# Attention with beacon tokens and an MLP on one core: values loaded straight to their rows, smaller first loads, and a fixed order of products per pair

## The chip, the cores and the metric

The kernel runs on one core of one Trainium2 chip. The metric is the device time of one execution in microseconds. An engine works through its own instruction list in order; engines meet through semaphores. The engines are TensorE (PE, matrix products), VectorE (DVE), ScalarE (ACT), GpSimd (POOL, which also issues the loads that change fp32 into fp16) and SyncE (SP, which issues the other DMAs).

## The reference

There are 8 batches of 8 heads, 576 tokens each, head width 64, and 16 beacon keys and values ahead of the tokens of each head. After the attention, an MLP (512 to 2048 to 512) runs over the 4608 tokens.

```python
k_all = np.concatenate([beacon_k, k], axis=2)      # 592 keys
v_all = np.concatenate([beacon_v, v], axis=2)
scores = scale * np.matmul(q, k_all.transpose(0, 1, 3, 2))
scores = np.where(causal, -1000000000.0, scores)   # beacons always seen
a = softmax(scores)
attn = np.matmul(a, v_all)
x = attn.transpose(0, 2, 1, 3).reshape(B * S, H * D)
h = x @ w_in
out = (h * (1.0 / (1.0 + np.exp(-1.702 * h)))) @ w_out
```

## The kernel before, in words

**Attention.** A step is one pair of heads of one batch: 32 steps. Scores are computed transposed, keys on the partitions (five blocks of 128 rows, the beacons being the first 16), in four chunks per pair (`qk_chunk`, L346). ACT takes the exponential of each chunk into an fp16 tile `E` (L364; two of them), and POOL or DVE clears the causal blocks. `av_half` (L413) multiplies by the values, four times per pair, into PSUM tiles `u` (four in the ring); the value tile holds ones beside the values, so the sums come out with the products. DVE or ACT evicts them to `O` (three); DVE alone turns the sums, takes reciprocals, turns them back, and multiplies into `xT` (L445 to L472).

**MLP.** Tokens are taken in nine groups of 512. The first layer has 16 tiles per group (`mlp1`, L489), each followed by a Gelu on ACT (L502), the second layer four tiles (`mlp2`, L512). ACT loads another table when it changes between exponential and Gelu. Group `g` becomes due behind step `ends[g]` (L806), 6, 10, 14 and so on.

**Queries and keys.** For batches 0 and 1 they are loaded six tokens to a row (`load_qk6`, L148) and transposed on PE (`tr_pe`, L174). For later batches they are loaded in another form (`load_qk`, L130), turned in squares on DVE (L273), put in order by DVE or POOL (L282), written to DRAM and read back in place by SP (L294 to L306).

**Values.** For batches 2 to 7 six DMAs per batch (`load_v`, L231) put each head's 64 values of a row straight in place. For batches 0 and 1 the values are loaded six tokens to a row into space that w_out will occupy later (`load_v6`, L160), and PE moves them to their rows with products against a 0/1 matrix (`v_pe`, L204; 30 products per batch and one for the beacons), which ACT or DVE evict (`v_pe_out`, L224). So three of the four loads of w_out wait for the last of these products (L702).

**The order.** Each piece of work is a `Work` with engines and estimated durations, a key, needs, and pieces that must be issued before it (`after`). `issue` (L849) simulates the engines: it takes again and again the piece that can start earliest, at equal times the one with the lowest key, and the instructions are then issued in that order. PSUM and SBUF tiles are handed out in rings (`Buf`, L551), so a piece may have to wait for the users of an older tile. Nothing but keys, needs and rings orders the products of PE among each other. Loads of later batches also wait for a step's first exponential (`late`, L706). Where the simulated PE would be idle in the first 60 us, it may put in warm-up products (`warm`, L914).

Of the kernel before, what the change touches and what calls it, by code (L numbers as in the profile page):

```python
# [16 lines left out]
def kernel(  # L17
# [11 lines left out]
    nc = tc.nc  # L29
# [22 lines left out]
    NBV = 2  # L52
# [27 lines left out]
    make_identity(nc, ident)  # L80
    keep = cst.tile([P, P + Nb], F16, tag="keep", name="keep")
    spread = cst.tile([TP, NKPAD + TR + 2], F16, tag="spread", name="spread")
    bkn = cst.tile([Nb, NB2, H, D], F16, tag="bkn", name="bkn")
    bvn = cst.tile([Nb, NBV, H, D], F16, tag="bvn", name="bvn")
# [13 lines left out]
    def make_spread():  # L98

        nc.gpsimd.affine_select(  # L100
            out=spread,
            in_=spread,
            compare_op=ALU.not_equal,
            fill=1.0,
            base=-Nb - TR,
            pattern=[[1, NKPAD + TR + 2]],
            channel_multiplier=-TR,
        )

# [9 lines left out]

# [3 lines left out]
    for t in kTs:  # L123
        nc.vector.memset(t[:, :, NK:NKPAD], 0.0)
# [21 lines left out]
    vflat = w2t.rearrange("p a n -> p (a n)")  # L146

    def load_qk6(b, g, w):  # L148
        if b not in nat6:
            nat6[b] = gp.tile([TP, 2, H, TR * D], F16, tag="g", name="g")  # L150
        nc.gpsimd.dma_start(
            out=nat6[b][:, w, g * HG : (g + 1) * HG, :],
            in_=(q, k)[w][b, g * HG : (g + 1) * HG].rearrange("h (p t) d -> p h (t d)", t=TR),
        )

    def v6(b):
        n = H * TR * D
        return vflat[0:TP, b * n : (b + 1) * n].rearrange("p (h t d) -> p h t d", h=H, t=TR)

    def load_v6(b):  # L160
        nc.gpsimd.dma_start(
            out=v6(b).rearrange("p h t d -> p h (t d)"),
            in_=v[b].rearrange("h (p t) d -> p h (t d)", t=TR),
        )

    def load_beacons(t, src):
        nc.gpsimd.dma_start(
            out=t.rearrange("n b h d -> n (b h) d"),
            in_=src[0 : t.shape[1]].rearrange("b h n d -> n (b h) d"),
        )  # L170
# [30 lines left out]

    vu = {}

    def v_pe(b, j):  # L204
        u = psu.tile([P, H * D], F32, tag="u", name="u")
        vu[(b, j)] = u
        if j == 0:
            nc.tensor.matmul(
                u[:, :],
                ident[0:Nb, :],  # L210
                bvn[:, b, :, :].rearrange("n h d -> n (h d)"),
                start=True,
                stop=False,
            )
        for t in range(TR):
            nc.tensor.matmul(  # L216
                u[:, :].rearrange("r (h d) -> r h d", h=H),
                spread[:, j * P - t + TR : (j + 1) * P - t + TR],
                v6(b)[:, :, t, :],
                start=(t == 0 and j > 0),  # L220
                stop=(t == TR - 1),
            )

    def v_pe_out(b, j, eng):  # L224
        r = min(P, NK - j * P)
        copy[eng](
            out=vbs[b % 2][0:r, j, :, 0:D],
            in_=vu[(b, j)][0:r, :].rearrange("r (h d) -> r h d", h=H),
        )

    def load_v(b, j, h0, h1):  # L231
        vb = vbs[b % 2]
        if j == 0:
            nc.gpsimd.dma_start(
                out=vb[0:Nb, 0, h0:h1, 0:D],
                in_=beacon_v[b, h0:h1].rearrange("h n d -> n h d"),
            )
            nc.gpsimd.dma_start(
                out=vb[Nb:P, 0, h0:h1, 0:D],
                in_=v[b, h0:h1, 0 : P - Nb, :].rearrange("h n d -> n h d"),  # L240
            )
        else:
            lo = j * P - Nb
            hi = min(lo + P, S)
            nc.gpsimd.dma_start(  # L245
                out=vb[0 : hi - lo, j, h0:h1, 0:D],
                in_=v[b, h0:h1, lo:hi, :].rearrange("h n d -> n h d"),
            )
# [311 lines left out]
    SEM = 0.1  # L560
# [10 lines left out]
    mkeep = Work("POOL", 0.3, -4.75, make_keep)  # L571
    mspread = Work("POOL", 1.0, -4, make_spread)
    beac = []

    def first_loads(b):
        k0 = 4 * b
        kl = -5 + 0.4 * b
        gb6 = Buf("g")
        lds = {}
        for g in range(2):  # L580
            for w in (1, 0):
                lds[(g, w)] = Work(
                    "POOL", 0.7, kl + 0.1 * g, lambda b=b, g=g, w=w: load_qk6(b, g, w),
                    alloc=gb6 if not lds else None, dma=1.8, after=list(lds.values())[:1],
                )
            if b == 0 and g == 0:
                for (t, src) in ((bkn, beacon_k), (bvn, beacon_v)):
                    beac.append(Work(
                        "POOL", 0.56, kl + 0.05, lambda t=t, src=src: load_beacons(t, src), dma=0.6,
                    ))  # L590
        ub = Buf("u")
        x = Work("PE", 0.3, k0, lambda b=b: tr_pe_beacon(b), beac[:1], alloc=ub)
        y = Work("DVE", 0.25, k0, lambda b=b: tr_pe_beacon_out(b), [x], alloc=kTb[b])
        use(ub, y)
        for p in range(NPAIR):
            for w in (1, 0):
                ub = Buf("u")
                kk = 4 * b + p - 0.5
                x = Work(
                    "PE", 0.55, kk, lambda b=b, p=p, w=w: tr_pe(b, p, w), [lds[(p // 2, w)]],  # L600
                    alloc=ub, after=[x],
                )
                use(gb6, x)
                z = Work(
                    dict(ACT=0.66, DVE=0.76), 0, kk,
                    lambda eng, b=b, p=p, w=w: tr_pe_out(b, p, w, eng),
                    [x], alloc=qTb[b] if (w, p) == (0, 0) else None,
                    after=[y] if w == 1 else [pk[(b, 0, 0)]] if p else (),
                )
                use(ub, z)  # L610
                pk[(b, p, w)] = z
        pk[b] = y

    def first_values(b):
        lv = Work("POOL", 0.8, -4.8, lambda b=b: load_v6(b), dma=3.6)
        for j in range(NJ):
            ub = Buf("u")
            kk = 4 * b + 0.5
            x = Work("PE", 1.35, kk, lambda b=b, j=j: v_pe(b, j), [lv, mspread] + beac[1:], alloc=ub,
                after=vpe[-1:],  # L620
            )
            V[(b, j)] = Work(
                dict(ACT=0.6, DVE=0.68), 0, kk,
                lambda eng, b=b, j=j: v_pe_out(b, j, eng),
                [x], alloc=vbb[b] if j == 0 else None, after=[V[(b, 0)]] if j else (),
            )
            use(ub, V[(b, j)])
            vpe.append(x)

    vpe = []  # L630
    for b in range(B):
# [5 lines left out]
        for g in range(2) if b >= NB2 else ():  # L637
            for w in (1, 0):
# [3 lines left out]
                    "POOL", 0.9, k0 - 1.5, lambda b=b, g=g, w=w: load_qk(b, g, w), alloc=nb_,  # L642
                    dma=1.8,
# [20 lines left out]
                if w == 1:  # L664
                    if bkB is None:
                        bkB = [
                            Work("POOL", 0.6, 4.3, lambda x=x: load_bk(x), after=[ld_], dma=0.7)
# [21 lines left out]
        if b < NBV:  # L689
            first_values(b)  # L690
            continue
        for j in range(NJ):
            V[(b, j)] = Work(
                "POOL", 0.9 + 0.6 * (j == 0), (4 * b - 1.5 if b >= NB2 else -3.9) + 0.1 * j,
                lambda b=b, j=j: load_v(b, j, 0, H),
                alloc=vbb[b] if j == 0 else None, after=[V[(b, 0)]] if j else (), dma=2.2,
            )
    for c in range(4):
        W1.append(Work("POOL", 0.75, -4 + 0.01 * c, lambda c=c: load_w1(c), dma=3.0))
        W2.append(Work(  # L700
            "POOL", 0.75, 4.2 + 0.01 * c, lambda c=c: load_w2(c),
            vpe[-1:] if 2 * c < 3 * NBV else [], dma=3.0,  # L702
# [17 lines left out]
    BIAS = 0.7  # L720
    avs = []
    evs = {}
    for i in range(NSTEP):
# [5 lines left out]
        for c in range(len(CH)):  # L729
# [9 lines left out]
            qks[(i, c)] = [qk_]  # L739
# [22 lines left out]
        for x in range(2):  # L762
            for half in range(2):
# [9 lines left out]
                avs.append(av)  # L773
                use(Eb, av)
# [31 lines left out]
    ends = [min(NPAIR * (((g + 1) * GT - 1) // S) + LAG, NSTEP) for g in range(NG)]  # L806
    gb = {}
    prev = []
    for g in range(NG):
# [3 lines left out]
        k0 = ends[g] - 0.4 + 2 * max(0, g - 7)  # L813
        for n in range(NNT):
# [5 lines left out]
            )  # L820
            for b in bs:
# [12 lines left out]
        for n in range(GT // P):  # L834
            u_, o_ = Buf("u"), Buf("osb")
            k1 = k0 + 1 + n
            m = Work("PE", 3.46, k1, lambda g=g, n=n: mlp2(g, n), gl + W2, alloc=u_)
            use(gb[g], m)
# [6 lines left out]
            use(o_, ot)  # L845
    for n in range(FILL):
        Work("PE", 0.22, 1e6, lambda: warm(), alloc=Buf("u"))

    def issue():  # L849
        free = dict(PE=1.0, ACT=1.0, DVE=2.0, POOL=1.0, SP=0.7)  # L850
# [5 lines left out]
        while todo:  # L856
            best = None
            for w in todo:
# [11 lines left out]
                if w.alloc is not None:  # L870
                    had = given[w.alloc.ring]
                    if len(had) >= rings[w.alloc.ring]:
# [3 lines left out]
                        t = max([t] + [x.t1 + SEM for x in old.users])  # L876
                for a in w.after:
                    t = max(t, a.t0)
                eng = min(w.opts, key=lambda e: max(t, free[e]) + w.opts[e] + (BIAS if e == 'ACT' and t > FILLT - 15 else 0))
                t = max(t, free[eng])  # L880
                c = (t, 0 if w.mode == mode == 1 else 1, w.key)
# [16 lines left out]
            if w.dma:  # L898
                dma_free[eng] = max(dma_free[eng], t + d + 0.7) + w.dma
                w.t1 = dma_free[eng] + (1.0 if t < 12 else dict(SP=4.0, POOL=2.0)[eng])  # L900
# [7 lines left out]
    nc.vector.memset(keep, 65504.0)  # L908
    nc.vector.memset(spread, 0.0)
    nc.vector.memset(bks, 0.0)  # L910
    wu = cst.tile([P, GT], F16, tag="wu", name="wu")
    nc.vector.memset(wu, 0.0)

# [37 lines left out]
```

The softmax here doesn't subtract the row's maximum and nothing guards it: scores larger than these inputs give would overflow.

## Time and profile before

| | us |
|---|---|
| median of six runs | 385.09 (383.93 to 386.06) |
| the profiled execution | 386.06 |
| its span | 384.4 |
| first transpose on PE | 8.65 |
| first attention product | 22.53 |
| first MLP product | 47.65 |
| table loads for Gelu | 47.89, 94.26, 133.72, 172.95, 212.50, 252.27, 291.32, 325.42 |

The span runs from the first to the last instruction of the profile. In the rows of slices each digit is the busy share of a fortieth of the span (9.6 us) in tenths, and for PEclk the clock granted to PE. In listings, `u<-E,vb` reads "writes u from E and vb", L425 is line 425 of the kernel, `x14` a count of instructions, and square brackets hold the idle time of the engine ahead of the instruction with what released it.

### The profile page before, as it was taken

The numbers are of one execution on the slowest core, as the hardware profiler recorded it, in microseconds if no ns is written. First come the engines' busy times: TensorE is split into PE (matmuls) and PEld (weight loads), VectorE is DVE, ScalarE is ACT, GpSimd is POOL, SyncE is SP. The second block draws the span as 40 slices with busy tenths as digits, with TensorE's granted clock in tenths as the row PEclk, the third lists the DMA queues.
The fourth block names the chain that finished last, engine by engine and source line by source line (L and its number), as shares of the span: only waits on it lengthen the run. The fifth ranks groups of instructions, "written<-read, shape, count | busy, mean of one in ns | idle before, by whom it ended". The sixth has DMA issues, their size and how long they took to land.

```text
span 384.4 us, 6119 instructions
## 1 busy us (share of the span) xinstructions
PE 367.6 (96%) x2328; PEld 180.9 (47%) x2328; DVE 266.5 (69%) x443; ACT 226.3 (59%) x334; POOL 146.5 (38%) x263
## 2 busy tenths in 40 slices
PE   7897999879999999999999999999999999999995
PEld 3453445434445444444445774545444544444442
DVE  6468999389977997699859985998595458000021
ACT  1776866627674767477746766586649563735300
POOL 9455772426533752466235724472321030000000
PEclk9998999989999999999999999999999999999999
DMA  8999998746955794669465947494400011000012
GB/s 117 202 206 143 138 181 117 170 135 115 128 142 136 142 130 128 148 116 148 128 158 94 157 110 186 89 144 112 142 27 30 0 56 45 11 27 27 14 69 82
DMA packets 60892, 42.79 MB, mean 111 GB/s; under 512 B 32192, under 2 KB 53184, under 8 KB 60864
## 3 DMA queue, kind: packets, MB, share of 16 engines
q0 software_dynamic: 42816, 18.62, 40.7%
q1 hardware_dynamic: 18048, 23.79, 20.1%
q8 instruction: 18, 0.29, 0.3%
q14 instruction: 10, 0.08, 0.1%
HBM read 44.40 MB, written 16.61 MB: 159 GB/s over the span
## 4 chain that ended last, share of the span: by engine, by line
PE 55%; DVE 28%; ACT 7%; DMA 5%; issue 3%; POOL 0%; SPq 0%; ACTq 0%; DVEq 0%
PE u L494 28%; PE u L516 16%; DVE xT L467 6%; DVE zt L448 6%; DVE O L436 5%; PE u L425 5%; ACT E L368 4%; DMA n<-in_k_dram 4%; PE s L355 3%; DVE sq L277 3%; DVE rz L458 3%; ACT L368 2%; DVE osb L529 2%; PE u L216 2%; PE u L916 2%
## 5 line engine op out<-in xcount | busy, mean ns | idle before, releaser
L368 ACT ACTIVATE E<-s 128x1024 f16<-128x1024 f32 (+3 forms) x128 | 104.0, 867 | 60.9 <-PE s L355 35.4
L494 PE MATMUL u<-xT,w 128*128 128x512 f16 (+1 forms) x640 | 133.6, 358 | 2.5 <-DVE O L436 1.6
L516 PE MATMUL u<-w,g 128*128 128x512 f16 x576 | 131.0, 383 | 3.3 <-DVE O L436 3.3
L506 ACT ACTIVATE g<-u 128x512 f16<-128x512 f32 x144 | 83.9, 598 | 53.0 <-PE u L494 52.9
L391 POOL TENSOR_SCALAR_AFFINE_SELECT E<-E 128x256 f16<-128x256 f16 (+2 forms) x147 | 58.5, 415 | 132.3 <-ACT E L368 131.8
L494 PEld LDWEIGHTS <-w 128*128 128x128 f16 x640 | 60.1, 98 | 60.1 <-issue 6.7
L516 PEld LDWEIGHTS <-g 128*128 128x128 f16 x576 | 55.0, 98 | 69.4 <-issue 5.9
L529 DVE COPY osb<-u 128x512 f32<-128x512 f32 x30 | 20.4, 681 | 74.8 <-PE u L516 74.6
L425 PE MATMUL u<-E,vb 128*128 128x336 f16 (+4 forms) x448 | 56.4, 269 | 0.8 <-DVE qT L187 0.7
L436 DVE COPY O<-u 128x240 f32<-128x240 f32 (+1 forms) x103 | 42.2, 432 | 14.9 <-PE u L425 13.4
L467 DVE TENSOR_TENSOR xT<-O,rz 64x576 f16<-64x576 f32 x64 | 51.8, 810 | 0.8
L448 DVE STREAM_TRANSPOSE zt<-O 64x576 f32<-64x576 f32 x64 | 49.3, 770 | 1.7 <-ACT O L436 0.2
L425 PEld LDWEIGHTS <-vb 128*128 128x128 f16 (+1 forms) x448 | 38.7, 99 | 20.7 <-issue 4.6
L355 PE MATMUL s<-qT,kT 64*128 64x80 f16 (+5 forms) x384 | 39.2, 285 | 3.8 <-ACT E L368 2.5
L286 POOL COPY t<-sq 128x576 f16<-128x576 f16 x24 | 29.0, 1210 | 32.6 <-DVE sq L277 32.1
L277 DVE STREAM_TRANSPOSE sq<-n 128x576 f16<-128x576 f16 x48 | 35.2, 752 | 5.3 <-DMA n<-in_k_dram 4.9
L355 PEld LDWEIGHTS <-kT 64*128 64x128 f16 x384 | 14.3, 94 | 33.1 <-issue 25.6
L286 DVE COPY t<-sq 128x576 f16<-128x576 f16 x24 | 27.3, 1137 | 0.2
L458 DVE STREAM_TRANSPOSE rz<-rt 128x576 f32<-128x576 f32 x32 | 24.4, 763 | 0.5
L245 POOL DMA_DIRECT2D vb<-in_v_dram x24 | 21.3, 893 | 0.0
L216 PE MATMUL u<-w,spread 96*128 96x512 f16 x60 | 13.6, 380 | 0.0
L436 ACT COPY O<-u 128x336 f32<-128x336 f32 (+1 forms) x25 | 10.4, 423 | 2.3 <-PE u L425 2.2
(49 smaller groups left out, 128.7 us busy)
## 6 DMA issues: line engine op xcount, KB each, us to landing
out_dram<-osb SPq DMA_DIRECT2D x36, 256.0 KB
d<-t SPq DMA_DIRECT2D x24, 148.0 KB
kT<-d SPq DMA_DIRECT2D x12, 296.0 KB
n<-in_k_dram POOLq DMA_DIRECT2D x12, 288.0 KB, 4.3
n<-in_q_dram POOLq DMA_DIRECT2D x12, 288.0 KB, 5.4
d<-t SPq DMA_DIRECT2D x24, 144.0 KB
qT<-d SPq DMA_DIRECT2D x12, 288.0 KB
vb<-in_v_dram POOLq DMA_DIRECT2D x18, 128.0 KB, 5.9
```

The source lines that it names most:

```text
L277: nc.vector.transpose(sqs[(b, g, w)][:, c * n : (c + 1) * n, :, :], nat[(b, g, w)][:, c * n : (c + 1) * n, :],)
L286: copy[eng](out=tqk[(b, g, w)][:, e, o : o + S].rearrange("p (r t) -> p r t", t=TPP), in_=sqs[(b, g, w)][:, :, e, :].rearrange("p t r -> p ...
L355: nc.tensor.matmul(sc[:, x, o : o + e - a], kT[r : r + 64, p, j * P : (j + 1) * P], qT[r : r + 64, p, a:e], start=True, stop=True,)
L368: nc.scalar.activation(out=Es[i][:, :, choff[ci] : choff[ci] + w], in_=scs[(i, ci)][:, :, 0:w], func=AFT.Exp, scale=0.125,)
L391: nc.gpsimd.affine_select(out=blk, in_=blk, compare_op=ALU.is_ge, fill=0.0, base=mc, pattern=[[0, 2], [1, w]], channel_multiplier=-1,)
L425: nc.tensor.matmul(u[:, lo:hi], vb[0:kw, j, :, :].rearrange("r h c -> r (h c)")[:, o : o + 2 * D], E[0:kw, x, col : col + hi - lo], start= ...
L436: copy[eng](out=Os[i][:, x, AQ[half] : AQ[half + 1]], in_=avu[(i, x, half)][:, :])
L448: nc.vector.transpose(zst[i][0][64 * x : 64 * x + 64, :, :], Os[i][64 * (1 - x) : 64 * (1 - x) + 64, x, :])
L467: vec[eng].tensor_tensor(out=xT[r : r + 64, p, c : c + S], in0=Os[i][r : r + 64, x, :], in1=zst[i][2][r : r + 64, :], op=ALU.mult,)
L494: nc.tensor.matmul(u[:, o : o + w], w1t[:, kp, nt * P : (nt + 1) * P], xT[:, kp, m : m + w], start=(kp == 0), stop=(kp == NKP - 1),)
L506: nc.scalar.activation(out=gts[g][:, nt, :], in_=hu[(g, nt)][:, :], func=AFT.Gelu_apprx_sigmoid)
L516: nc.tensor.matmul(o[:, :], gts[g][:, nt, mt * P : (mt + 1) * P], w2t[:, nt, :], start=(nt == 0), stop=(nt == NNT - 1),)
```

## The change

Values of all batches go through `load_v`. `load_v6`, `v_pe`, `v_pe_out`, the 0/1 matrix `spread` and the beacon value tile are gone, and the loads of w_out no longer wait for the spread products. The first loads of batch 0 are cut to heads 0 and 1, 2 and 3, 4 to 7, and batch 1 comes in one load for q and one for k. The identity is made behind the first loads. The simulated durations of loads are changed, at most eight DMAs of a queue may be under way in the simulation, and the preference between ACT and DVE depends on the time. MLP groups become due one step later (7, 11, 15 up to 31, then 32 twice). `chain` fixes the order of PE: the score chunks follow each other; the first-layer tiles of a group stand together behind a pair's last score; then each pair has two chunks, one second-layer tile, two chunks, and the four products of the pair before.

```diff
-    NBV = 2
-    make_identity(nc, ident)
-    spread = cst.tile([TP, NKPAD + TR + 2], F16, tag="spread", name="spread")
-    bvn = cst.tile([Nb, NBV, H, D], F16, tag="bvn", name="bvn")
...
-    def load_qk6(b, g, w):
+    def load_qk6(b, h0, h1, w):
...
+    def load_v(b, j):
         vb = vbs[b % 2]
+        lo = max(0, j * P - Nb)
+        hi = min((j + 1) * P - Nb, S)
+        r = Nb if j == 0 else 0
         if j == 0:
+            nc.gpsimd.dma_start(
+                out=vb[0:Nb, 0, :, 0:D], in_=beacon_v[b].rearrange("h n d -> n h d")
+            )
+        nc.gpsimd.dma_start(
+            out=vb[r : r + hi - lo, j, :, 0:D],
+            in_=v[b, :, lo:hi, :].rearrange("h n d -> n h d"),
+        )
...
-    SEM = 0.1
+    SEM, QS = 0.1, 0.1
...
-    mkeep = Work("POOL", 0.3, -4.75, make_keep)
-    mspread = Work("POOL", 1.0, -4, make_spread)
+    mkeep = Work("POOL", 0.3, -4.95, make_keep)
+    midn = Work("POOL", 0.6, -5.95, lambda: make_identity(nc, ident))
+    bk6 = Work("POOL", 0.57, -5.97, load_bk6, dma=0.25)
...
-        kl = -5 + 0.4 * b
+        kl = (-6, -4.4)[b]
...
-        for g in range(2):
+        for (h0, h1) in ((0, 2), (2, 4), (4, H)) if b == 0 else ((0, H),):
             for w in (1, 0):
...
-        if b < NBV:
-            first_values(b)
-            continue
+        kv = 4 * b - 1.5 if b >= NB2 else (-5.5, -3)[b]
...
         W2.append(Work(
-            "POOL", 0.75, 4.2 + 0.01 * c, lambda c=c: load_w2(c),
-            vpe[-1:] if 2 * c < 3 * NBV else [], dma=3.0,
+            "POOL", 0.78, 4.2 + 0.01 * c, lambda c=c: load_w2(c), dma=2.55,
             after=[Lq[(2, 1, 0)]],
         ))
...
-    BIAS = 0.7
+    BIAS = dict(DVE=0.5), dict(ACT=0.7)
...
-            qks[(i, c)] = [qk_]
+            qk_.after += list(qks.values())[-1:]
+            qks[(i, c)] = qk_
...
-    ends = [min(NPAIR * (((g + 1) * GT - 1) // S) + LAG, NSTEP) for g in range(NG)]
+    ends = [7, 11, 15, 19, 23, 27, 31, 32, 32]
...
-        k0 = ends[g] - 0.4 + 2 * max(0, g - 7)
+        k0 = ends[g] - 1 + 2 * max(0, g - 7)
...
+    def chain(*ws):
+        for x, y in zip(ws, ws[1:]):
+            y.after.append(x)
+
+    for g in range(NG):
+        e, nxt = ends[g], (ends + [NSTEP])[g + 1]
+        if e == NSTEP:
+            break
+        chain(qks[(e - 1, 3)], *m1s[g])
+        seq = [m1s[g][-1]] + avp[e - 1][:2] + [m2s[(g, 0)], qks[(e, 2)], qks[(e, 3)]]
+        seq += avp[e - 1][2:]
+        for i in range(e + 1, nxt):
+            seq += [qks[(i, 0)], qks[(i, 1)], *([m2s[(g, i - e)]] if i < e + 4 else []), qks[(i, 2)], qks[(i, 3)]]
+            seq += avp[i - 1]
+        if nxt < NSTEP:
+            seq.append(m1s[g + 1][0])
+        else:
+            seq += avp[nxt - 1] + [m2s[(g, 3)]]
+        chain(*seq)
...
-        free = dict(PE=1.0, ACT=1.0, DVE=2.0, POOL=1.0, SP=0.7)
+        free = dict(PE=1.0, ACT=1.0, DVE=1.0, POOL=0.7, SP=0.7)
+        landed = dict(POOL=[0.0] * 8, SP=[0.0] * 8)
...
-                        t = max([t] + [x.t1 + SEM for x in old.users])
+                        t = max([t] + [x.t1 + SEM + QS * w.mode for x in old.users])
...
+                if w.dma:
+                    t = max(t, landed[eng][-8])
```

## The prediction

> **What bounds the kernel now.** I read the page's engine shares, then its row of slices, then busy time by stage, and last the order of time in the first stage.
>
> ```profile
> span 384.4 us, 6119 instructions
> PE 367.6 (96%) x2328; PEld 180.9 (47%) x2328; DVE 266.5 (69%) x443; ACT 226.3 (59%) x334; POOL 146.5 (38%) x263
> PE   7897999879999999999999999999999999999995
> PEclk9998999989999999999999999999999999999999
> ```
>
> TensorE (PE) is busy 96% of the span: time is gained by giving PE less to do or by removing its gaps. The gaps and both dips of its clock lie in the first 80 us. Busy time by stage; the stages end at the first transpose, the first MLP product, the second MLP group, the last table load, the end (columns: length, PE, PEld, DVE, ACT, POOL, clock, DMA share, GB/s):
>
> ```profile
> 0.00:8.65 8.65, 6.13 (x18) 2.23 (x18) 5.87 (x8) 1.28 (x1) 7.80 (x18) 1.00 0.83 110
> 8.65:47.65 39.00, 35.30 (x382) 19.32 (x381) 28.09 (x49) 30.22 (x49) 22.77 (x45) 0.96 1.14 174
> 47.65:94.02 46.37, 42.34 (x265) 19.74 (x262) 38.18 (x64) 25.63 (x37) 20.20 (x33) 0.96 0.79 141
> 94.02:325.68 231.66, 229.05 (x1418) 114.99 (x1418) 188.79 (x316) 149.18 (x217) 95.71 (x170) 1.00 0.61 113
> 325.68:384.40 58.72, 54.76 (x253) 24.65 (x252) 5.54 (x8) 20.05 (x33) 0.00 (x0) 1.00 0.11 41
> ```
>
> From 94 us on PE idles 2.6 of 232 us, so a gain must come from before 94. The first stage in order of time:
>
> ```profile
> 14.87 0.38 PE L208 MATMUL u<-bvn,ident 16*128 16x512 f16 x1
> 15.18 6.65 PE L216 MATMUL u<-w,spread 96*128 96x512 f16 x30
> 22.53 1.77 PE L425 MATMUL u<-E,vb 128*128 128x240 f16 x14
> 22.64 0.76 DVE L187 COPY kT<-u 128x576 f16<-128x576 f16 x1 [8.02 <-PE u L179]
> 78.80 5.18 PE L516 MATMUL u<-w,g 128*128 128x512 f16 x16 [3.14 <-DVE O L436]
> 77.67 0.78 DVE L277 STREAM_TRANSPOSE sq<-n 128x576 f16<-128x576 f16 x1 [3.90 <-DMA n<-in_k_dram]
> ```
>
> For 6.9 us PE does nothing but spread batch 0's values, and VectorE (DVE) stands idle 8.0 us behind it. The last two lines are the second gap: DVE waited in its queue for a load issued at 68.3, its evictions stood behind that wait, and PE got no PSUM buffer for 3.14 us.
>
> **What the Trainium skill says.** "DMA: Bandwidth & Descriptors", Specifications: full rate needs pieces of at least 512 B. The trace agrees: of 128-byte packets (a head's row of values as written) at most 947 land per us, 121 GB/s, while the 768- and 1024-byte packets of the first 36 us go at 200 to 206. Same page, Anatomy of one DMA: about 2 us of a DMA are fixed; here a 16 KB load took 3.6 us from issue to landing. "TensorE: Matmul & The Clock Gate", What's actually happening: an idle window of about 3.4 us halves PE's clock. Both gaps here were followed by 3.4 us at 0.50 (34 to 37 and 79 to 82 us), some 1.7 us lost each.
>
> **The change part by part.**
> *Removed:* 60 spread products and 2 beacon products, 13.6 + 0.8 = 14.4 us of PE; ten evictions (nine on ScalarE (ACT) at 586 ns, one on DVE at 647 ns: 5.9 us); the spread mask (0.74 us of POOL), two value loads (0.78 each). *Added:* two batches of values as 12 row loads, each batch 0.56 + 0.85 + 4 x 0.89 = 5.0 us of POOL issue, so POOL pays +7.7 us in a stage where it is busy 22.8 of 39: hidden. The 0.6 MB of a batch take 5.0 us at 121 GB/s instead of 3.0 at 200: +4 us of DMA for both.
>
> *The start.* The identity (0.75 us from 0.8 on) moves behind the first two loads, and these are half as large (144 KB: 0.7 us less each at 200 GB/s). Before, beacon keys issued at 3.03 landed 5.2 later and released the first transpose at 8.65. Now they are third, at about 2.2, behind half the bytes: landing 6.6 to 7. Gain 1.9 us.
>
> *Batch 0's values.* POOL issues k, q, beacon keys, identity, k, q, then the value loads at about 4.4 to 9.4. Landed 4 to 6 later: 13.5 to 15.5; I take 14.5. The first attention products stood at 22.53: 8 us earlier. ACT has only pairs 0 and 1 before them (two E buffers).
>
> *To the first MLP group.* It began 25.1 us after those products. Its place moves from behind pair 5 to behind pair 6: one pair more, 3.25 us of exps (104.0/32) and 1.7 of evictions on ACT while DVE has 4.2 (transposes 1.54 + 0.77, reciprocal 0.26, multiplications 1.6): +5 us. Away go the evictions of batch 1 (3 us over two engines: -1.5); the 7 us of spread products there fall on a PE that is no longer the limit. 14.5 + 25.1 + 5 - 1.5 = 43.1. Cross-check from DMA: q, k of two batches and w_in are 4.46 MB at 200 GB/s, 22.3 us, plus batch 0's values 5.0, from 3.2 us: 30.5; batch 1's values come behind them, 35.5, landed about 37. Pair 4's products would be ready at 14.5 + 4 x 5 = 34.5, so they wait 2.5; pair 6's exps need pair 4's E buffer: 39 + 3.3, again some 42 to 43. PE has about 26 us of work (7 pairs of scores at 1.2, 6 of products at 1.76, 14 transposes at 0.45) in those 36; the planner may lay warm-up products in the holes. I take **43**, bounds 39 and 48 (38 to 43 us of evenly filled ACT and DVE, none of their 19.7 idle us recovered).
>
> *First MLP period*, 46.37 before against 39.4 later (mean of the spacings 39.46, 39.23, 39.55, 39.77 and 39.05). The excess is the gap, 3.14 + 1.7, some 1.3 of transposes, and 0.8. The load that came late was tied to pair 6's first exp, which lay behind the gelus; with the group behind pair 6 that exp, and the load, come before them: the gap goes. What is late next: pair 8's scores move from 83.9 to about 43 + 14 + 6.3 = 63, and batch 2's q and k must be transposed on DVE, written to DRAM and read back by then (their place DMAs stood at 63.0 and 67.6). DVE was 97% busy from 40 to 69 but has 8 us of early idle to give. I charge 2.5 us of waiting (bounds 0 and 9). While PE waits there, all later tiles wait too, since the order is fixed. Period: 39.0 + 0.9 (last transposes) + 2.5 = **42.4**.
>
> *The fixed order.* The period has 16 first-layer tiles, 4 second-layer tiles and 4 pairs. A step is now scores, one second-layer tile (3.6 us), scores, four products: 6.25 us. Row-mode changes stay four per pair. First-layer tiles come unbroken: 60 products took 12.95 us in the tail, so 16 tiles 13.8, where the broken block took about 14.45. ACT has 3.25 of exps and 0.4 to 0.9 of evictions in a step of 6.25; DVE 4.2 + 0.7 + most of the 1.7: near its limit, as before. The added waits put nothing behind them but PE's own order; the cover of each is the 3.6 us tile, without which a chunk's exp (1.0 us) would show. Gain taken 0.4 of the possible 0.65, loss bounded by the rival below: 5 x **39.0** = 195.
>
> *The end.* Group 6 starts one pair later, so 34.1 - 3.1 = **31.0** to group 7, and the tail of 58.7 is unchanged: groups 7 and 8 have the same tiles and the second-layer weights are long there (their loads, three of which waited for the last spread product until 45.2, only get earlier).
>
> **Sum.** 43 + 42.4 + 195 + 31.0 + 58.7 = 370.1 of span, against 384.4. The profiled execution took 386.06, 1.66 outside its span, and the six runs' median is 0.97 below it: 370.1 + 1.66 - 0.97 = **370.8 us**. Cross-check by PE: 367.6 - 14.4 - 3.4 (half clock) - 6.1 (warm-up at the start) = 343.7 of useful work; plus start 6.7, front holes 10, other gaps 4 and the 4.0 after the last product: 368.
>
> **Rivals.**
> *A, the front was hiding behind DVE and DMA* (chance 0.23): 14 us less of PE only uncovers them. Straight loads are slower; batch 1's values land at 42, not 37, or batch 2's rows are late by 9, with a half-clock stretch. For: DVE's 97% from 40 to 69, and batch 2's last value load, which took 23.2 us to land. Against: its 8 idle us. 370.8 + 5 + 4: 375 to 383, at 378.
> *B, everything packs* (0.17): front 39.5, no wait in the first period, 0.6 saved per period: 361 to 366, at 364.
> *C, the fixed order stalls in each step* (0.12), the case on the other side. A score or a second-layer tile needs its PSUM buffer evicted by a DVE that is at its limit, and nothing may pass it. From group 0 to the end there are 25 steps; 14.3/25 = 0.57 us a step cancels the gain, above that it is slower. At 0.8 a step: 391. Against: with a similar order, PE's waits in all of 94 to 326 are 2.6 us.
> *D, no change* (0.02): front and order cancel.
>
> **How the numbers follow.** The forecast's own case has 0.46, at 366 to 375. It and B lie below 0.3% of 385.1 (1.2 us, about what can be told from no change), so does nearly all of A: faster 0.86; same 0.03; slower 0.11. The range 362 to 382 leaves out C, D and the edges of A and B, under 2 in 10.
>
> **What would show it.** First transpose at 6.5 to 7 us; first attention products at 13.5 to 15.5, with DVE's 8.0 us wait gone; first MLP table load at about 43; the second about 42 later, then every 39.0; PE busy near 350 plus any added warm-up products. A first table load after 48, or PE waits on L355 or L516 of over 0.3 us in each step after 94 us, would make the prediction wrong.

## The result, and the profile after

The changed kernel took 384.77 us (median of 35 runs, 382.46 to 386.07) beside 385.06 for the kernel before on the same chips: ratio 1.0019, 95% interval 1.0002 to 1.0037. Every ratio here leaves out runs that lie over 1.5% above the fastest of the same kernel (here 21 of the 72 of the kernel before), so it can lie on the other side of 1 than the two medians. The forecast was 370.8. TensorE (PE) has lost the 14.4 us of products that the change takes away, and the time has not moved. The profiled execution took 383.71 us, its span is 382.0.

The page of the changed kernel: span, engine shares, PE's slices, the clock, and the packets:

```profile
span 382.0 us, 6021 instructions
PE 357.0 (93%) x2283; PEld 177.0 (46%) x2283; DVE 253.5 (66%) x421; ACT 233.1 (61%) x347; POOL 155.6 (41%) x269
PE   8967789479999999999999999999999999999995
PEclk9977999979999999999999999999999999999999
DMA packets 68716, 42.79 MB, mean 112 GB/s; under 512 B 41552, under 2 KB 61008, under 8 KB 68688
```

PE's first ten slices, which held 7s to 9s before, now hold a 6 and a 4: what was taken from PE came back as holes. PE's busy time fell by 10.6 us and not by 14.4, since more of it runs at half clock and the planner puts in 35 warm-up products (L863) where there were 18 (L916). Packets under 512 bytes rose from 32,192 to 41,552. Busy time by stage, cut at the first transpose, the first, second and sixth Gelu table load and the end; then two stretches out of the second and third stage (columns as in the table of stages before):

```profile
0.00:6.50 6.50, 5.24 (x12) 1.66 (x13) 4.54 (x7) 1.28 (x1) 5.26 (x14) 1.00 0.61 71
6.50:51.32 44.82, 34.68 (x394) 19.08 (x394) 31.27 (x55) 34.76 (x57) 33.91 (x59) 0.89 1.49 161
51.32:99.10 47.78, 39.16 (x234) 18.64 (x233) 35.22 (x62) 26.27 (x38) 26.59 (x41) 0.93 1.04 169
99.10:253.42 154.32, 153.44 (x1000) 79.67 (x999) 132.86 (x220) 107.33 (x157) 78.20 (x132) 1.00 0.75 138
253.42:382.00 128.58, 124.48 (x650) 57.94 (x648) 49.63 (x81) 63.43 (x95) 11.67 (x26) 1.00 0.13 44
19.44:22.60 3.16, 0.00 (x2) 0.00 (x0) 1.33 (x2) 0.04 (x1) 1.32 (x2) 1.00 1.30 204
70.84:78.75 7.91, 0.00 (x0) 0.03 (x1) 5.70 (x11) 0.48 (x2) 2.86 (x5) 0.76 0.38 121
```

Against the forecast's sum: the first table load stands at 51.3 and not at 43 (+8.3), the first MLP period is 47.8 and not 42.4 (+5.4), the next four take 154.3 and not 156 (-1.7), the end 128.6 against 31.0 + 58.7 + 39 = 128.7 (-0.1). That is +11.9, the difference of 382.0 and 370.1. From 99 us on the forecast holds, and all of the miss lies ahead of it. The two stretches are PE's largest waits there; PE in order of time:

```profile
14.22 2.19 PE L359 MATMUL u<-E,vb 128*128 128x240 f16 x14
22.60 0.29 PE L359 MATMUL u<-E,vb 128*128 128x208 f16 x2 [3.16 <-POOL E L325]
78.75 1.01 PE L289 MATMUL s<-qT,kT 64*128 64x512 f16 x8 [7.91 <-DMA qT<-d]
```

**The mask at 22.6.** POOL in order of time shows why a mask of 0.43 us is late. The first two lines are the loads of batch 1's keys and queries, the last one is ACT's: the exponentials that the mask needs.

```profile
11.45 0.81 POOL L130 DMA_DIRECT2D g<-in_k_dram  x1
12.23 0.81 POOL L130 DMA_DIRECT2D g<-in_q_dram  x1
18.29 0.84 POOL L179 DMA_DIRECT2D vb<-in_v_dram  x1 [0.29 <-DMA g<-in_q_dram]
21.23 0.89 POOL L179 DMA_DIRECT2D vb<-in_v_dram  x1 [2.09 <-DMA g<-in_k_dram]
22.12 0.43 POOL L325 TENSOR_SCALAR_AFFINE_SELECT E<-E 128x256 f16<-128x256 f16 x1
24.05 0.89 POOL L179 DMA_DIRECT2D vb<-in_v_dram  x1 [1.50 <-DMA g<-in_q_dram]
16.78 1.36 ACT L302 ACTIVATE E<-s 128x928 f16<-128x928 f32 x2
```

The value load at 21.23 was not issued before batch 1's keys had landed (9.5 us after their issue at 11.45), the one at 24.05 not before its queries had (11.5 us after 12.23). In both cases the load that is waited for is the eighth before, counted in POOL's own order, and so it is for each of the eight issues at which POOL waits for a DMA between 15 and 35 us: eight loads were under way, and the next one had to wait. POOL stands for 2.09 us, and the mask, whose exponentials had ended at 18.14, stands behind it and ends at 22.55.

PE's 3.16 us without work are followed by 6.8 us of half clock, from 23.7 us on. Another 3.4 us of it, from 33.9 on, come behind a second hole (31.2 to 34.4), in which PE was busy for 1.04 of 3.20 us and waited longest, 1.51 us, for a copy by ACT. The Trainium skill, "TensorE: Matmul & The Clock Gate", What's actually happening, has the clock halved after an idle window of about 3.4 us. The trace agrees in kind, but less than a whole idle window was enough: 3.16 us of idling in the first hole, and no more than 1.51 us in one piece in the second.

**The queries at 78.8.** SP in order of time; SPq marks an issue, and the same line serves keys and queries:

```profile
49.24 1.24 SPq L231 DMA_DIRECT2D d<-t  x2
63.60 0.41 SPq L237 DMA_DIRECT2D kT<-d  x1
64.07 5.55 SPq L231 DMA_DIRECT2D d<-t  x4
74.50 0.38 SPq L237 DMA_DIRECT2D qT<-d  x1
```

Batch 2's keys, written from 49.24 on, could be read back only at 63.60; in between the loads of w_out and of batch 2's values kept the DMA engines busy. The queries' writes stood behind that in SP's queue, and the queries were placed at 74.50. Pair 8's scores waited 7.91 us, while the DMA engines were busy for only 0.38 of the time (last row of the table above), and 6.9 us followed at a clock of 0.78.

### The profile page after: what moved, and what is told of

The parts are those of the page before. It is cut to its first block, busy times and chain, and to the rows that moved or that the text cites. A ratio compares the mean times of both kernels' runs of the same rounds, so it can differ in the third digit from the quotient of the medians.

```text
span 382.0 us, 6021 instructions
## 1 busy us (share of the span) xinstructions
PE 357.0 (93%) x2283; PEld 177.0 (46%) x2283; DVE 253.5 (66%) x421; ACT 233.1 (61%) x347; POOL 155.6 (41%) x269
## 4 chain that ended last, share of the span: by engine, by line
PE 67%; DVE 16%; DMA 4%; issue 2%; ACT 2%; SPq 0%
PE u L428 29%; PE u L450 27%; PE u L359 7%; PE s L289 5%; DVE zt L382 3%; DVE xT L401 3%; DMA d<-t 3%; DVE O L370 3%; DVE t L220 2%; DVE rz L392 1%; ACT E L302 1%; DVE sq L211 1%; DMA qT<-d 1%; DVE osb L463 1%; DVE rt L388 0%
## 5 line engine op out<-in xcount | busy, mean ns | idle before, releaser
L302 ACT ACTIVATE E<-s 128x1024 f16<-128x1024 f32 (+3 forms) x128 | 103.7, 864 | 48.3 <-PE s L289 46.4
L428 PE MATMUL u<-xT,w 128*128 128x512 f16 (+1 forms) x640 | 126.5, 358 | 0.4 <-DVE O L370 0.4
L440 ACT ACTIVATE g<-u 128x512 f16<-128x512 f32 x144 | 85.3, 597 | 44.4 <-PE u L428 44.1
L325 POOL TENSOR_SCALAR_AFFINE_SELECT E<-E 128x256 f16<-128x256 f16 (+2 forms) x150 | 66.0, 457 | 93.7 <-ACT E L302 93.4
L428 PEld LDWEIGHTS <-w 128*128 128x128 f16 x640 | 62.1, 98 | 61.4 <-issue 1.6
L370 DVE COPY O<-u 128x240 f32<-128x240 f32 (+1 forms) x88 | 36.8, 439 | 32.4 <-PE u L359 29.5
L401 DVE TENSOR_TENSOR xT<-O,rz 64x576 f16<-64x576 f32 x64 | 50.3, 786 | 0.9
L289 PE MATMUL s<-qT,kT 64*128 64x80 f16 (+5 forms) x384 | 37.5, 291 | 12.8 <-DMA qT<-d 7.9
L220 POOL COPY t<-sq 128x576 f16<-128x576 f16 x19 | 24.3, 1285 | 44.9 <-DVE sq L211 44.9
L179 POOL DMA_DIRECT2D vb<-in_v_dram x40 | 34.6, 870 | 5.6 <-DMA g<-in_k_dram 2.1
L370 ACT COPY O<-u 128x336 f32<-128x336 f32 (+1 forms) x40 | 15.8, 426 | 10.4 <-PE u L359 10.4
L461 ACT COPY osb<-u 128x512 f32<-128x512 f32 x7 | 4.1, 586 | 15.5 <-PE u L450 15.5
```

The lines of the kernel that those rows point to most:

```text
L220: copy[eng](out=tqk[(b, g, w)][:, e, o : o + S].rearrange("p (r t) -> p r t", t=TPP), in_=sqs[(b, g, w)][:, :, e, :].rearrange("p t r -> p ...
L289: nc.tensor.matmul(sc[:, x, o : o + e - a], kT[r : r + 64, p, j * P : (j + 1) * P], qT[r : r + 64, p, a:e], start=True, stop=True,)
L302: nc.scalar.activation(out=Es[i][:, :, choff[ci] : choff[ci] + w], in_=scs[(i, ci)][:, :, 0:w], func=AFT.Exp, scale=0.125,)
L325: nc.gpsimd.affine_select(out=blk, in_=blk, compare_op=ALU.is_ge, fill=0.0, base=mc, pattern=[[0, 2], [1, w]], channel_multiplier=-1,)
L370: copy[eng](out=Os[i][:, x, AQ[half] : AQ[half + 1]], in_=avu[(i, x, half)][:, :])
L401: vec[eng].tensor_tensor(out=xT[r : r + 64, p, c : c + S], in0=Os[i][r : r + 64, x, :], in1=zst[i][2][r : r + 64, :], op=ALU.mult,)
```

## The experiments

All runs do the whole computation unless the text says otherwise. T1 and T2 are the first and second table load for Gelu; in the changed kernel 51.3 and 99.1. They are read from one execution each, the time and the ratio from all runs. Every edit goes through the planner, which may draw the whole order anew: with e1's edit, for instance, it puts in 42 warm-up products in place of 35 and moves transposes on PE. Where little else moved, the text says so.

### Is PE's removed work worth anything?

The changed kernel with the old way of the values put back (`load_v6`, `v_pe`, `v_pe_out`, `spread` and w_out's wait for the last spread product, as in the listing before), for both batches, and then for batch 1 alone.

```diff
+    PEV = (0, 1)        # e12;  (1,) in e3
...
+        if b in PEV:
+            first_values(b, kv)
+            continue
```

> The changed kernel with the values of both batches by the old way, so that of the change only the smaller first loads, the fixed order and the planner's numbers are left. PE has 14.4 us more to do, the DMA engines some 4 us less and POOL eight DMAs less. By my prediction's sum 383 to 386 (only the fixed order's 0.4 to 0.8 us per period and 2 us at the start left). With batch 1 alone so it took 382.3: if the DMA theory holds, 380 to 386, no worse than the changed kernel although PE has 14.4 us more.

383.57 us, ratio to before 0.9974 (0.9949 to 1.0000). T1 56.5, T2 100.9. Its page:

```profile
PE 365.7 (96%) x2332; PEld 180.9 (47%) x2332; DVE 252.6 (66%) x419; ACT 235.6 (62%) x353; POOL 157.4 (41%) x268
```

PE does 14.4 us of products more (with 22 warm-up products in place of 35), and the kernel is no slower. The edit also takes nine loads out of POOL's queue and brings larger packets, so it shows a balance: what straight values save on PE, they cost elsewhere.

> The changed kernel with batch 1's values by the old way (one load of 576 KB, 30 spread products, evictions), batch 0's straight to their rows. It puts 7 us of PE work and 3 us of evictions back and takes four DMAs out of POOL's queue. Queue theory: first Gelu table load at 45 to 47, time 377 to 381. If PE is what counts (my prediction's sum of PE work), it is 5 to 7 us slower than the changed kernel: 389 to 392.

382.28, ratio 0.9948 (0.9922 to 0.9974), T1 53.0, T2 96.6. With one batch spread by PE its small packets are gone, POOL issues two loads in place of six and w_out comes later; by T2 these were together worth 2.5 us more than the 7 us of products cost.

### Is the fixed order the loss?

```diff
-            qk_.after += list(qks.values())[-1:]
...
-    for g in range(NG):
+    for g in ():
```

> The changed kernel with no fixed order on PE (no chains, groups still due at 7, 11 and so on). Theory that the fixed order is harmless and saves 0.5 to 0.8 us per period: period of the Gelu table loads 39.2 to 39.6 instead of 38.6, time 386 to 389. Rival that the fixed order stalls: period below 38.6, time 378 to 382.

401.05, ratio 1.0463 (1.0404 to 1.0522). T1 51.1 as with the order, then periods of 51.6, 41.3, 41.0, 42.2 and 42.4. PE's two largest waits in the whole run (line, releaser: sum, number, longest):

```profile
PE u L428 <- DVE O L370: 10.0, 5, 3.7
PE s L289 <- ACT E L302: 7.4, 10, 0.9
```

With the rest of the new plan kept, the order is worth some 16 us. It does not cost, so the rival of stalls in each step falls.

### Masks, SP's order, batch 2's loads: three single edits

Masks of pairs 0 to 5 on DVE alone; SP's place of batch 2's keys behind the writes of the queries; batch 2's first q and k loads ahead of batch 1's values.

```diff
-                dict(DVE=0.46 * nm, POOL=0.41 * nm), 0, i + 0.3,                                        # e1
+                dict(DVE=0.3 * nm) if i < 6 else dict(DVE=0.46 * nm, POOL=0.41 * nm), 0, i + 0.3,
...
+                if b == 2 and w == 0 and g == 0:       # e5
+                    kpl.after += wr
...
-                    "POOL", 0.56, k0 - 1.5, lambda     # e2
+                    "POOL", 0.56, k0 - 1.5 if (b, g) != (2, 0) else -3.5 + 0.1 * (1 - w), lambda
...
-                late.append((Lq[(b, g, w)], 4 * b + 2 * g - 6))
+                late += [(Lq[(b, g, w)], 4 * b + 2 * g - 6)] if (b, g) != (2, 0) else []
```

> The changed kernel with the causal masks of pairs 0 to 5 on DVE alone, so that no mask stands in POOL's queue behind a value load that waits for one of eight DMA slots. Queue theory: the 3.16 us wait of PE for a mask at 19.4 and the half clock after it go, the first Gelu table load comes at 46 to 48 instead of 51.3, the time falls by 3 to 5 us to 380 to 382. Theory that DVE and ACT work bounds the first stage: DVE gets 6 to 8 us more there, table load at 53 or later, time 386 to 388.

389.68, ratio 1.0133 (1.0057 to 1.0210). T1 46.4 is 4.9 us earlier, although this execution started slowly: half clock from 8.4 to 15.2 us put its first attention product at 17.61 (14.22 in the changed kernel). From that product to T1 it takes 28.8 us; the changed kernel takes 37.1, and the forecast had 28.5. But T2 is 100.6: pair 8 still waited for its queries, 8.2 us, until 76.2.

> The changed kernel with one constraint more on SP: the place DMA of batch 2's first k rows is issued behind the writes of the q rows instead of ahead of them. In the changed kernel it stood in SP's queue from 50.5 to 63.6, waiting for its own writes, with the q writes behind it. Theory that this queue order delays batch 2's q: pair 8's wait falls from 7.9 to about 3 us, time 378 to 381. If the writes themselves are slow because the DMA engines are full until 63, the wait stays at 7 to 8 and so does the time, 384 to 386.

392.1, ratio 1.0200 (1.0148 to 1.0252). The queries are placed at 69.02 (74.50 before the edit), pair 8's wait falls to 5.3, and T2 is 107.2: waits of 3.2 and 2.2 us for evictions and 17 us of half clock come behind it. Here nothing else moved: PE, ACT and DVE issue the same instructions in the same order as in the changed kernel.

> The changed kernel with the q and k loads of batch 2's first four heads issued right behind the w_in loads, ahead of batch 1's values. Theory of the late rows: the 7.9 us wait of pair 8's scores for the place DMA of batch 2's q and the 6.8 us of half clock around it shrink to under 2 us; time 376 to 380, if the later values of batch 1 do not cost more than 2 us. If the rows are late because of POOL and SP queues and not because of the load, the wait stays above 6 us and the time is 384 to 387.

392.4, ratio 1.0239 (1.0165 to 1.0312). The wait for the queries is gone, T2 is 108.7. PE's longest waits:

```profile
PE u L359 <- DVE osb L463: 7.6, 1, 7.6
PE u L450 <- DVE O L370: 3.7, 2, 3.5
PE u L450 <- DMA w<-in_moe_w_out_dram: 3.4, 2, 2.8
PE u L359 <- POOL E L325: 2.7, 2, 1.7
```

Each edit removed or shortened the wait at which it was aimed, and each kernel was slower: another wait stood in the same 40 us. The first two together:

> Both queue edits on the changed kernel: masks of pairs 0 to 5 on DVE, and batch 2's k place behind the q writes. With the masks alone the first Gelu table load came 4.9 us earlier (46.39) and pair 8 then waited longer (8.2 us and 10.2 us of half clock). If the place order is the cause of that wait, pair 8's scores come at 70 to 72 instead of 76.2 and the time is 376 to 380; if the rows are bound by their loads and writes, 384 to 390 as with the masks alone.

391.44, ratio 1.0192 (1.0126 to 1.0258): T1 44.1, T2 106.4, pair 8 waits 11.1 us until 75.7. This is no new pair, though. With e1's edit the planner had already put the keys behind the queries' writes, and e6 issues the same instructions as e1, on every engine in the same order. So these are two executions of one program, and they show how far T1 and T2 can be trusted: T1 differs by 2.3 us, T2 by 5.9. The stretch from the first attention product to T1 differs by less, 28.8 and 29.7 us.

### Fewer bytes

The weights' first half is loaded and used twice, so that 2.1 MB of fp16 are not written; the second half of both matrices is left out of the computation. The number of products is unchanged. The kernel before got the same edit as a control.

```diff
-    for c in range(4):
+    for c in range(2):
         W1.append(...)          # and W2 alike
...
-            w1t[:, kp, nt * P : (nt + 1) * P]
+            w1t[:, kp, nt % 8 * P : (nt % 8 + 1) * P]
```

> The changed kernel with half of each weight matrix loaded and used twice: 2.1 MB fewer as written (10.5 us of DMA at 200 GB/s), four DMAs fewer, the same instructions on PE, ACT and DVE; it leaves out the other half of w_in and w_out. Theory that the DMA engines bound the first 75 us: first Gelu table load at 46 to 48, no wait of pair 8 over 3 us, time 372 to 378. If queue order on POOL and SP is what costs, whatever the bytes, the waits stay and the time is 382 to 386.

> Control: the kernel before with half of the weights loaded and used twice (it leaves out the other half). DMA theory: its first 48 us are full of PE work, so it gains less than the changed kernel, 0 to 5 us (the late load at 68 to 78 us may go): 379 to 385. If it gains as much as the changed kernel does, the DMA engines were the limit of both and the change did not make them one.

375.28, ratio 0.9755 (0.9689 to 0.9821), against 382.0, ratio 0.9941 (0.9912 to 0.9969), for the control: 9.5 us from the changed kernel, 3.1 from the kernel before. T1 50.4 is nearly unchanged, T2 is 92.2: the first period is 41.7, and the waits for queries are gone. So 2.1 MB, and the four loads that carry them in POOL's queue, weigh more after the change than before it.

> The changed kernel with half of each weight matrix loaded and used twice, and the masks of pairs 0 to 5 on DVE; it leaves out the other half of w_in and w_out. Two-cause theory: first Gelu table load at 44 to 46 (masks no longer behind waiting loads), second at 86 to 88 (no late rows), time 368 to 372, the sum of my prediction. If only the DMA bytes count, 374 to 377 as with half the weights alone.

The same with e1's masks: 374.05, ratio 0.9719 (0.9645 to 0.9794), T1 47.2, T2 90.5. Of the 3.3 us gained by T1, 1.6 are left at T2; the two intervals overlap.

### The same bytes in the order of their use

Batch 1's values, then batch 2's first q and k (which, as in e2, no longer wait for a step's first exponential), then w_in. e10 does it with half the weights.

```diff
-        kv = 4 * b - 1.5 if b >= NB2 else (-5.5, -3)[b]
+        kv = 4 * b - 1.5 if b >= NB2 else (-5.5, -4.2)[b]
...
-        W1.append(Work("POOL", 0.75, -4 + 0.01 * c, ...
+        W1.append(Work("POOL", 0.75, -3.5 + 0.01 * c, ...
...
-                    "POOL", 0.56, k0 - 1.5, lambda
+                    "POOL", 0.56, k0 - 1.5 if (b, g) != (2, 0) else -3.7 + 0.1 * (1 - w), lambda
```

> The changed kernel with only the order of the first loads changed: batch 1's values, then batch 2's first q and k, then w_in (2.1 MB as written, 10.5 us of DMA that nothing needs before the first MLP product). Load theory: batch 1's values land by 27 instead of 40, batch 2's rows are placed before 60, pair 8 does not wait; first Gelu table load at 44 to 47, time 370 to 376. If DVE and ACT work bounds the first stage, the table load stays at 50 or later; with pair 8's wait gone alone the time is 376 to 380.

385.0, ratio 1.0018 (0.9988 to 1.0048), T1 51.8, T2 99.6. Pair 8 no longer waits, and the time is the same. DVE's longest wait, and what PE waited for after it, in order of time:

```profile
74.52 0.78 DVE L211 STREAM_TRANSPOSE sq<-n 128x576 f16<-128x576 f16 x1 [7.53 <-DMA n<-in_k_dram]
85.30 4.94 PE L450 MATMUL u<-w,g 128*128 128x512 f16 x16 [4.25 <-DVE O L370]
```

DVE stands 7.5 us at a load of batch 3, needed four pairs later. Evictions stand behind it; that PE's 4.25 us come from there is tested below.

> Half of the weights loaded, as in the run before, and the loads of batch 1's values and batch 2's first q and k ahead of w_in. It leaves out the other half of w_in and w_out. DMA theory: no late rows at all, second Gelu table load at 88 to 92 instead of 99, time 368 to 375, near the sum of my prediction. Queue theory: 380 to 386, as with the load order alone (385.0).

376.47, ratio 0.9785 (0.9723 to 0.9846): with half the weights the order of loads makes no clear difference to e9's 375.28. With masks on DVE the full-weight kernel was the second slowest of all (e5's edit stands in it too, and changes nothing in its order):

> The load order of the run before and the masks of pairs 0 to 5 on DVE, so that POOL issues loads without masks between them. If masks behind waiting loads still count with the better load order, 2 to 4 us faster than that run, 368 to 373; if DVE is now the limit of the first stage, 2 to 5 us slower than it.

394.58, ratio 1.0265 (1.0212 to 1.0318); PE waited 9.7 us for an `O`.

### Both: batch 1 by PE and its loads ahead of w_in

e3's edit with batch 1's load and w_in in e7's places.

> All work done: the changed kernel with batch 1's values in one load and spread by PE, and that load ahead of w_in. Batch 1's spread products (7 us) then fall between 20 and 35 us, where PE had holes, and the DMA engines carry 2 us less. DMA theory: first Gelu table load at 47 to 50 instead of 53 with the late load, time 376 to 380. If w_in then comes late or the rows of batch 2 do, 382 to 386.

379.32, ratio 0.9843 (0.9769 to 0.9917), T1 50.6, T2 95.9. PE's spread products lie in holes from 29 to 39 us, and the clock of the first stage is 1.00 (0.89 in the changed kernel's second row). PE waits 4.6 us for an `O` at 74.1, and DVE stands before that:

```profile
68.97 1.44 DVE L272 STREAM_TRANSPOSE sq<-n 128x576 f16<-128x576 f16 x2 [9.77 <-DMA n<-in_k_dram]
```

Two edits on top of it, batch 2's loads early and masks on DVE:

> As the run before, with batch 2's first q and k loads ahead of w_in as well. With the rows early and the DMA engines relieved: 374 to 379. If, as in the earlier load order of this kind, the next loads (batch 3's, behind w_out) then come late and DVE stands in front of them: 382 to 387.

> As e14 with the masks of pairs 0 to 5 on DVE. If masks behind waiting loads still cost in that order: 3 us below e14; if the first stage is then bound by DVE, or batch 2's rows come late all the same, equal to e14 or up to 5 us above.

388.2, ratio 1.0095 (1.0067 to 1.0124), with a wait of 9.6 us for an `O`; and 379.39, ratio 0.9883 (0.9793 to 0.9972), no gain. In e16's profiled execution (383.83, the slowest of its four) PE waited 5.2 us for a mask on DVE, and T1 came at 54.7, later than without the edit.

### The wait in DVE's order

After e9 my theory was that the DMA engines are simply short of time until 75 us, and that each mended wait must come back elsewhere. DVE's stand in e7 and e14 is another reading: the transposes of batch 3's first group stand ahead of work that needs no bytes. The edit puts those transposes later in DVE's order, on e14 (e17) and on e7 (e18). The planner moves what hangs on them: copies on POOL, writes and places on SP. PE's order of products stays in e17 as in e14, and in e18 as in e7 but for two pieces; POOL's loads come in the same order.

```diff
+                if (b, g) == (3, 0):
+                    sq3 += tr
...
+    for x in sq3:
+        x.after.append(norms[6][1])
```

> The kernel with batch 1's values spread by TensorE and its loads ahead of w_in, and in addition the transposes of batch 3's first group placed, in VectorE's order, behind the multiplications of pair 6 instead of ahead of pairs 6 and 7. All of the work is done. In the kernel without this edit VectorE stood 9.8 us (59.2 to 69.0) for the load of that group, TensorE then waited 4.6 us for an O at 74.1 and ran 6.8 us at half clock: 8.0 us in all, at 379.3. Theory (what is left in the first 75 us is a wait for bytes that lands on whatever stands in the way; here it stands on VectorE's queue, and nothing behind it needs that load): VectorE's stand is under 3 us, no wait of TensorE over 2 us before the second Gelu table load, second table load at 89 to 93, time 371 to 375. Rival (the bytes are late for something needed as well): batch 2's rows or w_out take over, TensorE waits over 3 us elsewhere before 100, second table load at 95 or later, 378 to 385.

> The changed kernel (all values straight) with its loads in the order batch 1's values, batch 2's first queries and keys, w_in, and the same edit of VectorE's order: the transposes of batch 3's first group behind pair 6's multiplications. All of the work is done. Without that edit it took 385.0, with VectorE standing 7.5 us for that load (to 74.5) and TensorE waiting 4.25 us at 85.3, and second table load at 99.6. Theory that the stand was only where a shortage of bytes showed: straight values fill the engines of the DMA for longer, so some other wait of 3 us or more comes in its place (w_out's second-layer tiles, batch 2's rows, a mask), second table load at 97 or later, time 382 to 388. Rival (the wait in VectorE's order is the cause, the bytes would be there in time): no wait over 2 us after 55 us, second table load at 91 to 94, time 376 to 380, near or below the kernel that spreads batch 1's values on TensorE.

e17: 376.61, ratio 0.9788 (0.9727 to 0.9850), T2 93.5. e18: 379.07, ratio 0.9853 (0.9809 to 0.9898), T2 93.3. Between e18 and e7 DVE's order differs, with what hangs on it, and that is worth 5.9 us; from e14 to e17 it is 2.7, and the intervals overlap. e18 by stage (start to T1, T1 to T2), then PE's longest wait in the second of them:

```profile
0.00:51.34 51.34, 39.54 (x402) 20.59 (x403) 37.39 (x63) 36.53 (x61) 39.84 (x70) 0.87 1.41 160
51.34:93.30 41.96, 38.75 (x245) 18.70 (x244) 34.20 (x58) 26.45 (x39) 23.15 (x39) 1.00 1.10 166
86.31 0.60 PE L289 MATMUL s<-qT,kT 64*128 64x512 f16 x8 [3.06 <-DMA qT<-d]
```

With every byte and every straight load of the changed kernel, the first period is 41.96. So a mere shortage of bytes did not make it long: the bytes came in an order that did not fit the order in which engines stood for them. e9's gain does not speak against this: with half the weights the loads come earlier, and an order that did not fit before can fit. e17's stages to T1 and from T1 to T2:

```profile
0.00:51.57 51.57, 42.01 (x434) 21.77 (x435) 40.50 (x72) 37.31 (x61) 35.66 (x64) 0.97 1.25 165
51.57:93.48 41.91, 37.80 (x238) 17.95 (x236) 31.46 (x54) 26.67 (x40) 24.79 (x40) 1.00 1.03 157
```

In the first 51 us it does 7 us more of spread products than e18 (and seven warm-up products less), in the same time, at a clock of 0.97 instead of 0.87. e17 is the fastest full kernel here, 2.1% under the kernel before. Whether its values by PE or e18's straight ones are better is not settled: the medians differ by 2.5 us, and the intervals overlap.

## Why the prediction was wrong

**The start and batch 0's values: right.** First transpose 6.50 (6.5 to 7), first attention products 14.22 (14.5 taken), DVE's wait of 8.0 us gone.

**"To the first MLP group": the step that failed first, 51.3 instead of 43.** The sum ran over ACT, DVE and PE, and wrote POOL's +7.7 us of issue off as hidden because POOL was busy 22.8 of 39 us. It was the stage's share of POOL that was read, not its order: masks stand behind value loads in it. The prediction asked of each load when it lands, and not how long POOL would stand before it may issue it. V(1)'s last block, assumed landed at 37, was issued at 29.18 and landed 10.7 later, at 39.9. Measured: 3.16 us of PE's wait for a mask, with 6.8 us of half clock behind it, and from the first attention product to T1 37.1 us instead of 28.5. With masks off POOL this stretch is 28.8 and 29.7 (e1 and e6), so nearly all of the 8.3 lies there. The planner moved other work on PE along with the masks, so the wait's share alone is not shown. In kernels that keep masks on POOL, T1 stayed at 50 to 53 with straight values in any order of loads, and with half the weights.

**"First MLP period": the mechanism was right, its size was not.** The prediction named batch 2's rows as what is late next and charged 2.5 us, bounds 0 and 9. The wait was 7.9, and half clock followed it. It took DVE's idle time for the cover; the cover was missing on SP's queue, which stood until 63.6 for the keys' writes, beside loads. When load order and DVE's order fit (e18), the period is 41.96 against the 42.4 forecast. So those 5.4 us did not hang on PE's products; order brings them back.

**The premise under both.** "TensorE is busy 96%: time is gained by giving PE less to do." Before 80 us that does not follow: taking PE's work away uncovered waits of equal length, and e12 puts all 14.4 us back without being slower. Rival A said this (375 to 383, chance 0.23) and was nearest, but it saw the first stage's loss in V(1) landing at 42, where it landed at 39.9 and a mask was late. The loss on the first two stages was 13.7 us instead of its 9, and so came the case that the forecast called "no change", at a chance of 0.02.

**A reading that was wrong, without weight.** Small packets landed at up to 1,072 per us (in the kernel before, from 256 us on), not "at most 947". A batch of values then takes 4.4 us instead of 5.0, which would have made the forecast lower still.

**The fixed order, the periods and the end: right.** Periods of 38.95, 38.26, 38.48 and 38.63 (39.0); PE idles 0.9 of 154 us; e4 prices the order.

**What stays open.** No run has both mends, masks off POOL and e18's order, so it is not shown that they add up; e8, e7's order with masks on DVE, took 394.58. In e1 and e6 pair 8's scores came at 76.2 and 75.7, close to the 78.8 of the changed kernel, so what T1 gained went into a longer wait for the queries; why the gain was lost in e8 is not worked out. In e16, with batch 1 by PE, masks on DVE made T1 later and not earlier. DVE's order alone, without the new order of loads, was not tried on the changed kernel.

## What to carry to other kernels

A share of busy time near 100% is not a bound where the work covers waits of other queues: before taking work from PE, ask for each later wait what else ends within the same few us, queue by queue, with the engine that *issues* a load among the queues. Loads want the order in which their bytes are used, and an engine's instructions want the order in which their loads land: the first alone gained nothing here (e7, 1.0018), both together 1.5% (e18, 0.9853). When three single mends each make a kernel slower, that is no proof against the waits they remove; look at who stands next, and, where a planner lays out the order, at what else it moved. And run one program twice before reading stages from a trace: here T2 of the same instructions differed by 5.9 us.

## What the runs showed of the hardware

POOL stands in order at a load that it may not issue yet: 2.09 us here, with a mask behind it that was ready; in each of eight such waits the eighth load before it had to land first. Two writes of some 148 KB from SP, issued at 49.24, were done at 63.6 beside the loads of w_out and of batch 2's values.

Half clock came, in all 20 traces, in stretches of 3.41 us or whole multiples of it, apart from those that a trace's start or end cuts off. Cut each trace into pieces of 3.41 us at these edges. A piece at full clock in which PE was busy for less than 0.43 of the time was always followed by half clock (28 pieces), one with more than 0.62 never (2,007); in between (40) it went both ways. So holes need not be whole to halve the clock. And less work for PE made it slower per product: with 7 us of spread products less, e18's mean clock over the span is 0.980, with 13.7 us of half clock before T1, and e17's is 0.995, with 3.4.
